# Attention values moved by 32 rows: sixteen transfers or sixty-four ScalarE copies

## The chip, the cores and the metric

The kernel runs on one core of a Trainium2 chip. The core has five instruction queues that run side by side and wait for each other through semaphores: TensorE (PE, matrix products), VectorE (DVE), ScalarE (ACT), GpSimd (POOL) and SyncE (SP, which here only issues transfers). Each queue works strictly in its own order. The metric is the device time of one execution in microseconds (us); lower is better.

## The reference

Two stages follow each other. The first is banded attention over 8 batches and 8 heads, 576 positions, head size 64. Heads 0 to 3 see the last 32 positions, heads 4 to 7 see 32 positions at a stride of 4. The second is a mixture of experts in which each of the 4608 tokens goes to one of 8 experts.

```python
mask_plain = (rel >= 0) & (rel < window)                                   # window = 32
mask_dil = (rel >= 0) & (rel < window * dilation) & (rel % dilation == 0)  # dilation = 4
attn = softmax(where(mask, q @ k.T / 8, -1e9)); x = attn @ v               # x: 4608 x 512
e_idx = argmax(x @ w_gate + modality_bias[modality_id])
out[t] = gate_w[t] * (relu(x[t] @ w1[e_idx[t]]) @ w2[e_idx[t]])
```

## The kernel before

**Attention.** The work is cut into 72 units, nine for each batch (`m` = 0 to 8). A unit computes 128 query rows of four heads; `kd` = 0 names the plain heads, `kd` = 1 the dilated ones. Units 0 to 3 are plain, unit 4 holds 64 rows of each, units 5 to 8 are dilated. A tile of 64 queries needs 96 keys: its own 64 and the 32 before them. The values of one batch and `kd` lie in a tile `vw` of 96 partitions: rows 32 to 95 of slot `i` hold the 64 values of tile `i`, rows 0 to 31 hold the last 32 values of tile `i - 1`. `load_v` (L123 to L132) fills rows 32 to 95 from device memory, with one transfer for `kd` = 0 and twelve for `kd` = 1. `shift_v` (L134) then fills rows 0 to 31 by moving rows 64 to 95 one slot on, inside the on-chip memory. Three `vw` tiles rotate.

**The loop.** At step `t` the loop (L940) emits, for each engine, pieces of several units: the scores of unit `t` (L340), the exponent of `t - 1` (L351), the transposed probabilities of `t - 2` (L356 on PE, the copy `pT` L359 on ACT), the product with the values of `t - 3` (`attend`, L365), the transposition of the result of `t - 4` (L387, `uxh` L391 on ACT, `uxl` L392 on DVE), the routing logits of `t - 5` (L411). In six of nine steps two `pieces` follow: transpositions of the next keys and queries (L294), which ACT copies out (L309, L311). PE, DVE, ACT and SP run in exactly this order; GpSimd's order is made by a scheduler, except for what goes through the object `pool`, which is kept in program order. The row-maximum subtraction `sm` runs there (L347, shown as L278, the helper's line).

**SP's queue.** Per batch it issues sixteen transfers of keys and queries (`st`, L116), thirteen of values (L127, L131) and two shifts (L137). The shift of `kd` = 1 is emitted at `m` = 3, that of the next batch's `kd` = 0 at `m` = 8.

**Routing.** After each batch a generator `gating` chooses the experts. Its product with `ewt` (L454) is a plain `nc.gpsimd` instruction, free to be placed by the scheduler. After batch 4 three expert slots of 256 tokens are full early. Their token rows are gathered by GpSimd (`xr`), go through device memory (`x_slot`, `xg`) and are transposed on DVE and split in two parts (`prepare_x`, L787 to L794).

**Mixture of experts.** `slots` (L817) runs 19 slots of eight blocks: products with `w1` (L855) and `w2` (L835), fed by splits of the weights on ACT and DVE (L803, L804). It starts in the step after the generator `background` has set `state['go']`, and is interleaved with the last attention units. That generator, for batch 4, gathers slot 0, runs `prepare_x`, waits for the last batch (`t` = 63), issues six groups of weight transfers, two yields apart, and then sets `go`. Since it is advanced twice a step, `prepare_x` before it delays what follows.

Of the kernel before, what the change touches and what calls it, by code (L numbers as in the profile page):

```python
# [15 lines left out]
ALU = mybir.AluOpType  # L16
# [6 lines left out]
B, H, S, D = 8, 8, 576, 64  # L23
# [4 lines left out]
WIN = 32  # L28
NCLS = 4
CL = S // NCLS  # L30
TQ = 64
NTILE = S // TQ
# [32 lines left out]
def kernel(  # L65
# [65 lines left out]
                nc.sync.dma_start(out=t[WIN + o:WIN + o + n, :, i, 0:D], in_=vv[r, j:j + n])  # L131
        return t  # L132

    def shift_v(b, kd):  # L134

        t = vw(b, kd)
        nc.sync.dma_start(out=t[0:WIN, :, 1:NTILE].rearrange("p h i d -> p h (i d)"),  # L137
                          in_=t[TQ:KW, :, 0:NTILE - 1].rearrange("p h i d -> p h (i d)"))

    state = {('qk', 0, 0): load_qk(0, 0, nc.scalar)}  # L140
    state['v', 0, 0] = load_v(0, 0)
# [20 lines left out]
    for m, kinds_of in enumerate(kinds):  # L162
        for u, kind in enumerate(kinds_of):
# [6 lines left out]
            if o is not None:  # L170
                mo = mt[:, 0:WIN + o]
                nc.gpsimd.affine_select(out=mo, in_=mo, pattern=[[0, WIN + o]], compare_op=ALU.is_ge,
                                        fill=-BIG, base=o - 1, channel_multiplier=-1)


    shift_v(0, 0)

    KC, FC = DM // P, FF // P
    w1q = [wraw.tile([P, KC, HALFF * P], F32, name=f"w1q{i}") for i in range(FC // HALFF)]
# [257 lines left out]
    def gating(b, lT):  # L437

        sh = [GB, NE, NGB]
        blk = slice(b * NGB, (b + 1) * NGB)  # L440
        lgp = psum['o'].tile([P, 512], F32, name="po")
        lg = lgp[0:GB, 0:NGB * 2 * NE].rearrange("p (c e) -> p e c", e=2 * NE)
        for c in range(NGB):
            nc.tensor.transpose(out=lg[:, :, c], in_=lT[:, GB * c:GB * (c + 1)], identity=ident[:2 * NE, :2 * NE])
        l = gwk.tile(sh, F32, name="l")
        nc.vector.tensor_tensor(out=l, in0=lg[:, 0:NE], in1=mterm[:, :, blk], op=ALU.add)
        nc.vector.tensor_tensor(out=l, in0=lg[:, NE:2 * NE], in1=l, op=ALU.add)
        mx = gwk.tile([GB, 1, NGB], F32, name="mx")
        nc.vector.tensor_reduce(out=mx[:, 0, :], in_=l.rearrange("p e c -> p c e"), op=ALU.max, axis=AX.X)
        mxb = mx.broadcast_to(sh)  # L450
        yield
        t0 = gwk.tile(sh, F32, name="t0")
        nc.vector.tensor_tensor(out=t0, in0=l, in1=mxb, op=ALU.is_equal)
        (nc.vector if b == B - 1 else nc.gpsimd).tensor_tensor(out=t0, in0=t0, in1=ewt, op=ALU.mult)  # L454
        ex = gwk.tile(sh, F32, name="ex")
        pool.tensor_tensor(out=ex, in0=l, in1=mxb, op=ALU.subtract)
        yield
        if b < B - 1:
            yield
        m2 = gwk.tile([GB, 1, NGB], F32, name="m2")  # L460
        nc.vector.tensor_reduce(out=m2[:, 0, :], in_=t0.rearrange("p e c -> p c e"), op=ALU.max, axis=AX.X)
        oh = gwk.tile(sh, BF16, name="oh")
        nc.vector.tensor_tensor(out=oh, in0=ewt, in1=m2.broadcast_to(sh), op=ALU.is_equal)
        nc.scalar.activation(out=ex, in_=ex, func=AF.Exp)
        yield
        sm_ = over_e(ex, "sume")
        pool.tensor_scalar(out=sm_, in0=sm_, scalar1=1e-9, scalar2=None, op0=ALU.add)

        rkp = psum['o'].tile([P, 512], F32, name="po")
        rk = rkp[0:GB, 0:NE * NGB].rearrange("p (e c) -> p e c", c=NGB)  # L470
        run = state['run']
        nc.tensor.matmul(out=rk, lhsT=upper, rhs=oh, start=True, stop=False)
        for c in range(NGB - 1):
            nc.tensor.matmul(out=rk[:, :, c + 1:], lhsT=ones_bf, rhs=oh[:, :, c:c + 1].broadcast_to([GB, NE, NGB - 1 - c]), start=False, stop=False)
        nc.tensor.matmul(out=rk, lhsT=ones_bf, rhs=run.broadcast_to(sh), start=False, stop=True)
        t1 = gwk.tile(sh, F32, name="t1")
        nc.vector.tensor_tensor(out=t1, in0=rk, in1=eoff, op=ALU.add)
        state['counts', b] = [run[:, :, 0]] + [oh[:, :, c] for c in range(NGB)]
        if b < B - 1:
            state['run'] = gwk.tile([GB, NE, 1], BF16, name="run")  # L480
            r3 = gwk.tile([GB, NE, 3], BF16, name="r3")
            pool.tensor_tensor(out=r3, in0=oh[:, :, 0:3], in1=oh[:, :, 3:6], op=ALU.add)
            for c in range(3):
                pool.tensor_tensor(out=state['run'], in0=run if c == 0 else state['run'], in1=r3[:, :, c:c + 1], op=ALU.add)
        yield
        pool.tensor_tensor(out=t1, in0=t1, in1=oh, op=ALU.mult)
        dst = gwk.tile([GB, NGB], I32, name="dst")
        yield
        nc.vector.tensor_copy(out=dst, in_=over_e(t1, "dstf"))
        nc.vector.reciprocal(out=pay[:, blk, 1].bitcast(F32), in_=sm_)  # L490
        scatters = state['scatters'] = []
        for c in range(NGB):
            if c > 0 and b < B - 1:
                yield
                if b not in round_of:
                    yield
            ins = nc.gpsimd.indirect_dma_start(out=table, out_offset=bass.IndirectOffsetOnAxis(ap=dst[:, c:c + 1], axis=0),
                                               in_=pay[:, b * NGB + c, :], in_offset=None).ins
            tc.add_manual_dep(ins, state['pool'].name, mybir.DependencyInfo(mybir.DependencyClass.NoSync, mybir.DependencyReason.SCHED_ONLY),
                              reason="GpSimd's order, but for the scatters among themselves")  # L500
            for before in scatters:
                tc.declare_no_dep(ins, before, reason="every token has a row of its own")
            for load in state['loads_of_ids']:
                tc.declare_no_dep(ins, load, reason="the rows of full slots are written before")
            scatters.append(ins)
        if b < B - 1:
            wait_all(scatters.pop(), scatters)
# [202 lines left out]
    def load_more(n, pieces):  # L710

        if n not in loads_of and n in si_of:
            loads_of[n] = [fetch_weights(si_of[n], n == 0), 0]
        if n in loads_of:
            for _ in range(min(pieces, 6 - loads_of[n][1])):
                next(loads_of[n][0], None)
                loads_of[n][1] += 1

    def background(b):


        if b < B - 1:
            yield
        steps = gating(b, state['lT', b])
        if b in round_of:
            for _ in steps:
                yield
                if ('counts', b) in state:
                    break
            yield from together(steps, slot_info(state['counts', b], round_of[b]))  # L730
            if round_of[b] > 0:
                return
            yield
            for n in range(2):
                fetch_slot(n)
                yield
            for _ in gather(0, ids_of[0]):
                yield
                yield
            for _ in range(4):  # L740
                yield
            yield from prepare_x(0, ids_of[0])

            while state['t'] < (B - 1) * 9:
                yield
            for _ in range(6):
                load_more(0, 1)
                yield
                yield
            while state['t'] < NU - 2:  # L750
                yield
            state['go'] = True
            return
        yield from steps
        if b == B - 1:
            yield
            yield from slot_info(state['counts', b], len(EARLY))
            yield from rest_info()
            state['routed'] = True
# [158 lines left out]
    for ch in qk_chunks(0, *state['qk', 0, 0]):  # L918
        ch()
    state['qk', 1, 0] = load_qk(1, 0)  # L920
    shift_v(0, 1)

    credit = 0.0

# [15 lines left out]
    for t in range(NU + LAG + 1):  # L940
# [10 lines left out]
        if t < NU:  # L951
            jobs = order[t][1]
            if m == 0:
                state['lT', b] = gwk.tile([2 * NE, S], F32, name="lT")
            if b + 1 < B:
                if m == 4:
                    pieces = qk_chunks(0, *state['qk', b + 1, 0])
                elif m == 8:
                    pieces = qk_chunks(1, *state['qk', b + 1, 1])
                    shift_v(b + 1, 0)  # L960
            if m == 0 and b > 0:
                load_v(b, 1, slice(6, None))
            elif m == 3:
                if b > 0:
                    shift_v(b, 1)
                if b + 1 < B:
                    state['v', b + 1, 0] = load_v(b + 1, 0)
            units.append(Unit(b, m, jobs, [state['v', b, 0], state['v', b, 1]] if m >= 4 else [state['v', b, 0]], state['lT', b]))
            units[t].scores()
# [20 lines left out]
        if 0 <= t - 4 < NU:  # L990
            units[t - 4].store()
            units[t - 4].keep(pool)
        for i in range(2):
            step()
            if i < len(pieces):
                pieces[i]()
# [56 lines left out]
```

## Time and profile before

| | |
|---|---|
| three timed executions | 732.46, 734.70, 734.91 us; median 734.7 us |
| the profiled execution | 731.71 us, of which 729.8 us is the span |
| first product of the mixture of experts | 279.55 us |
| last product of the mixture of experts | 711.5 us |
| mean granted TensorE clock | 0.926 |

The profile is one execution. A group's row reads: line, engine, operation, what it writes and reads, count, busy time, mean duration, and the idle time of the engine just before, with what ended it. A window's row gives, for a stretch of the span, each engine's busy time with its number of instructions, then the granted clock of TensorE as a share of full speed, the busy share of the transfer engines and the bytes they moved. A timeline row is start, duration, engine, line, operation and count, with the idle time before it in brackets. SP's rows are the times in which it was issuing.

### The profile page before, as it was taken

The page shows a single profiled execution, that of the slowest core. Times are in us where ns is not written, and L with a number is a line of the kernel's source. Part 1 is how long each engine was busy: PE and PEld are TensorE (multiplying, and loading weights), DVE is VectorE, ACT ScalarE, POOL GpSimd, SP SyncE. Part 2 cuts the span into 40 slices and gives each one's busy share as a digit, 9 for nine tenths or more (in the row PEclk, how much of TensorE's full clock was granted, in tenths as well). Part 3 has the DMA queues.
Part 4 walks back from the last instruction along what each step waited for, and adds up shares of the span by engine and source line. Part 5 has one row for each costly group of instructions (what it writes and reads, how often), then busy time and mean ns, then how long its engine had stood idle before and what let it go on. Part 6 is the DMA issues. An engine that isn't in the chain of part 4 may idle for free. (4 is left out here: it accounts for less than half of the span.)

```text
span 729.8 us, 17822 instructions
## 1 busy us (share of the span) xinstructions
PE 659.7 (90%) x6286; PEld 581.2 (80%) x6286; DVE 500.3 (69%) x1212; ACT 411.9 (56%) x900; POOL 292.1 (40%) x396
## 2 busy tenths in 40 slices
PE   5798789799687888989999999999999999999991
PEld 3686678687576767879999999998999999999980
DVE  1478579588586786786777666777666776667660
ACT  3476467477454544545656565566565666565550
POOL 7334557467465764564333133232132322220110
PEclk7599799799887868999999999999999999999996
DMA  9797796969967692423434583332323326831730
GB/s 161 134 220 174 161 197 154 211 141 188 185 140 165 183 239 76 101 73 111 123 95 124 169 223 87 102 116 74 102 73 102 116 75 164 239 92 54 189 93 12
DMA packets 165536, 99.20 MB, mean 136 GB/s; under 512 B 124400, under 2 KB 143346, under 8 KB 165444
## 3 DMA queue, kind: packets, MB, share of 16 engines
q1 hardware_dynamic: 148916, 68.15, 42.5%
q0 software_dynamic: 11120, 28.64, 12.8%
q10 hardware_dynamic: 5408, 1.24, 1.1%
q8 instruction: 51, 0.84, 0.5%
q14 instruction: 41, 0.34, 0.2%
HBM read 127.52 MB, written 29.39 MB: 215 GB/s over the span
## 5 line engine op out<-in xcount | busy, mean ns | idle before, releaser
L855 PE MATMUL pt<-xh,w1l 128*128 128x256 f32 (+1 forms) x608 | 172.5, 284 | 3.2 <-DVE w1l L804 3.2
L855 PE MATMUL pt<-xl,w1h 128*128 128x256 f32 (+1 forms) x608 | 172.3, 283 | 0.0
L855 PE MATMUL pt<-xh,w1h 128*128 128x256 f32 (+1 forms) x608 | 172.2, 283 | 0.1
L861 ACT ACTIVATE hh<-pt 128x256 fp32r<-128x256 f32 (+1 forms) x152 | 57.6, 379 | 165.7 <-PE pt L855 165.7
L278 POOL DMA_INDIRECT xr<-x_dram,idt x74 | 84.6, 1144 | 122.9 <-DMA x_slot<-xr 83.9
L804 DVE TENSOR_TENSOR w2l<-w2q,w2h 128x512 fp32r<-128x512 f32 x152 | 104.9, 690 | 41.3 <-ACT w2h L803 33.1
L855 PEld LDWEIGHTS pt<-xh,w1h 128*128 128x128 f32 x608 | 116.7, 192 | 7.0 <-ACT w1h L803 0.4
L855 PEld LDWEIGHTS pt<-xl,w1h 128*128 128x128 f32 x608 | 116.8, 192 | 5.7
L855 PEld LDWEIGHTS pt<-xh,w1l 128*128 128x128 f32 x608 | 116.6, 192 | 4.0 <-DVE w1l L804 4.0
L835 PE MATMUL py<-w2h,hh 128*128 128x512 f32 x296 | 117.6, 397 | 0.0
L835 PE MATMUL py<-w2h,hl 128*128 128x512 f32 x296 | 116.8, 395 | 0.0
L835 PE MATMUL py<-w2l,hh 128*128 128x512 f32 x296 | 116.0, 392 | 0.0
L862 DVE SCALAR_TENSOR_TENSOR hl<-pt,hh 128x256 fp32r<-128x256 f32 (+1 forms) x152 | 63.4, 417 | 75.7 <-ACT hh L861 75.6
L278 POOL DMA_INDIRECT out_dram<-ys,idt x37 | 39.2, 1059 | 177.7 <-ACT ys L838 115.0
L804 DVE TENSOR_TENSOR w1l<-w1q,w1h 128x512 fp32r<-128x512 f32 x152 | 103.9, 684 | 1.8 <-ACT w1h L803 1.7
L803 ACT CAST w1h<-w1q 128x512 fp32r<-128x512 f32 x152 | 94.5, 622 | 2.3 <-DMA w1q<-in_moe_w_dram 2.3
L803 ACT CAST w2h<-w2q 128x512 fp32r<-128x512 f32 x152 | 93.1, 612 | 0.1
L359 ACT COPY pT<-pt 96x512 f32<-96x512 f32 x72 | 41.8, 581 | 89.3 <-PE pt L356 88.3
L365 PE MATMUL po<-vw,pT 96*64 96x65 f32 x1152 | 58.3, 247 | 28.3 <-DMA vw<-vw 19.5
L278 POOL TENSOR_TENSOR sm<-sm,nmx 128x384 f32<-128x384 f32 x72 | 59.8, 831 | 55.6 <-DVE den L372 32.3
L365 PEld LDWEIGHTS po<-vw,pT 96*64 96x64 f32 x1152 | 46.7, 155 | 40.3 <-issue 13.9
L835 PEld LDWEIGHTS py<-w2l,hh 128*128 128x128 f32 x296 | 55.7, 188 | 13.2
(159 smaller groups left out, 1114.2 us busy)
## 6 DMA issues: line engine op xcount, KB each, us to landing
w2q<-in_moe_w_dram SPq DMA_DIRECT2D x76, 512.0 KB
w1q<-in_moe_w_dram SPq DMA_DIRECT2D x152, 256.0 KB
st<-in_k_dram SPq DMA_DIRECT2D x64, 144.0 KB
x_slot<-xr SPq DMA_DIRECT2D x18, 512.0 KB
xg<-x_slot SPq DMA_DIRECT2D x72, 128.0 KB
x_dram<-x_sb POOLq DMA_DIRECT2D x32, 256.0 KB
st<-in_q_dram SPq DMA_DIRECT2D x56, 144.0 KB
vw<-in_v_dram SPq DMA_DIRECT2D x8, 576.0 KB
```

Source lines behind the costliest of these rows:

```text
L278: ins = tc.keep_in_program_order(getattr(nc.gpsimd, name)(*args, **kw))
L359: nc.scalar.copy(out=self.pT, in_=src)
L365: nc.tensor.matmul(out=pov[u * TQ:(u + 1) * TQ, h, :], lhsT=self.pT[:, h, u * TQ:(u + 1) * TQ], rhs=self.vts[kd][:, h, i, :], start=True, ...
L803: nc.scalar.copy(out=hi, in_=raw)
L804: nc.vector.tensor_tensor(out=lo, in0=raw, in1=hi.bitcast(F32), op=ALU.subtract)
L835: nc.tensor.matmul(out=py[u], lhsT=ht[:, us], rhs=wt, start=(f + n == 0), stop=(f + n == FC + 1))
L855: nc.tensor.matmul(out=ph, lhsT=wt[:, c, :], rhs=xt[:, c, 0:cols], start=(c + i == 0), stop=(c + i == KC + 1))
L861: nc.scalar.activation(out=hh, in_=ph, func=AF.Relu)
L862: nc.vector.scalar_tensor_tensor(out=hl, in0=ph, scalar=0.0, in1=hh.bitcast(F32), op0=ALU.max, op1=ALU.subtract)
```

## The change

`shift_v` no longer issues a transfer. It copies the 32 rows of one head with one ScalarE instruction, and the loop calls it once per step, between `store` and the `pieces`: heads 0 to 3 of `kd` = 1 at `m` = 3 to 6, heads 0 to 3 of the next `kd` = 0 at `m` = 8, 0, 1 and 2 (for the first batch two heads at `t` = 0 and two at `t` = 1). The product with `ewt` goes through `pool`. In `background`, `prepare_x` no longer stands ahead of the weight transfers but beside their second half.

```diff
-    def shift_v(b, kd):
+    def shift_v(b, kd, h):
 
         t = vw(b, kd)
-        nc.sync.dma_start(out=t[0:WIN, :, 1:NTILE].rearrange("p h i d -> p h (i d)"),
-                          in_=t[TQ:KW, :, 0:NTILE - 1].rearrange("p h i d -> p h (i d)"))
+        nc.scalar.copy(out=t[0:WIN, h, 1:NTILE].rearrange("p i d -> p (i d)"), in_=t[TQ:KW, h, 0:NTILE - 1].rearrange("p i d -> p (i d)"))
...
-        (nc.vector if b == B - 1 else nc.gpsimd).tensor_tensor(out=t0, in0=t0, in1=ewt, op=ALU.mult)
+        (nc.vector if b == B - 1 else pool).tensor_tensor(out=t0, in0=t0, in1=ewt, op=ALU.mult)
...
             for _ in gather(0, ids_of[0]):
                 yield
                 yield
-            for _ in range(4):
-                yield
-            yield from prepare_x(0, ids_of[0])
 
             while state['t'] < (B - 1) * 9:
                 yield
-            for _ in range(6):
+            for _ in range(3):
                 load_more(0, 1)
                 yield
+                yield
+            steps = prepare_x(0, ids_of[0])
+            for i in range(6):
+                if i % 2 == 0:
+                    load_more(0, 1)
+                next(steps, None)
                 yield
...
+        if 3 <= m <= 6 and b < B:
+            shift_v(b, 1, m - 3)
+        elif t < NU and (m == 8 and b + 1 < B or m < 3):
+            for h in ((m + 1) % 9,) if t > 2 else {0: (0, 1), 1: (2, 3), 2: ()}[t]:
+                shift_v(b + (m == 8), 0, h)
```

The four calls of the old `shift_v` (ahead of the loop, at `m` = 3 and at `m` = 8) go. The instructions move in three places. First, ScalarE's queue in a batch from `m` = 3 on: the row maximum's exponent `pe`, the copy `pT`, `uxh`, and the key and query copies `kT`, `qT`. Before:

```order
L351 ACTIVATE pe<-sm 128x384
L359 COPY pT<-pt 96x512
L391 CAST uxh<-pt 128x256
L351 ACTIVATE pe<-sm 128x384
L359 COPY pT<-pt 96x512
L391 CAST uxh<-pt 128x256
L311 COPY kT_101<-pt 128x2x2x96
L309 ACTIVATE qT_100<-po 128x2x2x96
```

and with the change:

```order
L347 ACTIVATE pe<-sm 128x384
L355 COPY pT<-pt 96x512
L387 CAST uxh<-pt 128x256
L137 COPY vw_106<-vw_106 32x520
L347 ACTIVATE pe<-sm 128x384
L355 COPY pT<-pt 96x512
L387 CAST uxh<-pt 128x256
L137 COPY vw_106<-vw_106 32x520
L307 COPY kT_101<-pt 128x2x2x96
L305 ACTIVATE qT_100<-po 128x2x2x96
```

A copy now stands behind `uxh` in eight of nine steps, ahead of the key and query copies. The transfers of SP's queue keep their order without the shifts.

Second, GpSimd's queue in batch 6, where the routing of batch 5 meets the gathers `xr` of slot 0. The number of a tile grows with the place of its instruction in the program; `t0` is the product with `ewt`. Before:

```order
L278 TENSOR_TENSOR sm_4181<-sm_4181,nmx_4182 128x384
L454 TENSOR_TENSOR t0_4347<-t0_4347,ewt_268 96x48
L278 TENSOR_TENSOR ex_4350<-l_4304,mx_4307 96x48
L278 DMA x_dram0_84<-x_sb_4212 128x2x256
L278 DMA xr_4215<-x_dram0_84,idt_4146 128x256
L278 DMA x_dram1_85<-x_sb_4065 128x2x256
L278 TENSOR_TENSOR sm_4235<-sm_4235,nmx_4236 128x384
L278 DMA xr_4215<-x_dram1_85,idt_4146 128x256
L278 TENSOR_TENSOR sm_4310<-sm_4310,nmx_4311 128x384
```

and with the change:

```order
L274 TENSOR_TENSOR sm_4219<-sm_4219,nmx_4220 128x384
L274 DMA xr_4253<-x_dram0_84,idt_4184 128x256
L274 DMA x_dram1_85<-x_sb_4102 128x2x256
L274 TENSOR_TENSOR sm_4274<-sm_4274,nmx_4275 128x384
L274 DMA xr_4253<-x_dram1_85,idt_4184 128x256
L274 TENSOR_TENSOR sm_4350<-sm_4350,nmx_4351 128x384
L274 DMA xr_4253<-x_dram0_84,idt_4184 128x256
L274 TENSOR_TENSOR t0_4387<-t0_4387,ewt_267 96x48
L274 TENSOR_TENSOR ex_4390<-l_4344,mx_4347 96x48
```

The product stood ahead of two `sm` of earlier steps and stands behind them now; the first gather stands ahead of them.

Third, TensorE's queue at the end of attention: the last scores (`pss`), and the first products of the mixture of experts (`pt<-xh,w1h`). Before:

```order
L340 MATMUL pss<-kT_103,qT_102 64x96 x8
L365 MATMUL po<-vw_104,pT 64x65 x8
L411 MATMUL po<-uxh,wgs 16x128
L411 MATMUL po<-uxl,wgs 16x128
L411 MATMUL po<-uxh,wgs 16x128
L411 MATMUL po<-uxl,wgs 16x128
L356 MATMUL pt<-ident,pe 96x128 x4
L387 MATMUL pt<-ident,x_sb 128x128 x2
L365 MATMUL po<-vw_104,pT 64x65 x8
```

and with the change:

```order
L336 MATMUL pss<-kT_103,qT_102 64x96 x8
L361 MATMUL po<-vw_104,pT 64x65 x8
L407 MATMUL po<-uxh,wgs 16x128
L407 MATMUL po<-uxl,wgs 16x128
L407 MATMUL po<-uxh,wgs 16x128
L407 MATMUL po<-uxl,wgs 16x128
L854 MATMUL pt<-xh,w1h 128x256
L854 MATMUL pt<-xl,w1h 128x256
L854 MATMUL pt<-xh,w1l 128x256
```

The mixture of experts begins two steps earlier, in the step of the last scores: `go` is set at `t` = 70 instead of 72. The first weight transfers are issued at `t` = 63 instead of 66.

More of the change, by code (lines that the diff above doesn't have):

```diff
@@ L173 @@
                                         fill=-BIG, base=o - 1, channel_multiplier=-1)
-    shift_v(0, 0)
     KC, FC = DM // P, FF // P
@@ L920 @@
     state['qk', 1, 0] = load_qk(1, 0)
-    shift_v(0, 1)
     credit = 0.0
@@ L959 @@
                     pieces = qk_chunks(1, *state['qk', b + 1, 1])
-                    shift_v(b + 1, 0)
             if m == 0 and b > 0:
@@ L963 @@
             elif m == 3:
-                if b > 0:
-                    shift_v(b, 1)
                 if b + 1 < B:
```

## The prediction

> **What bounds the kernel now.** I read the page first, for the engines and the granted clock.
>
> ```profile
> span 729.8 us, 17822 instructions
> PE 659.7 (90%) x6286; PEld 581.2 (80%) x6286; DVE 500.3 (69%) x1212; ACT 411.9 (56%) x900; POOL 292.1 (40%) x396
> PEclk7599799799887868999999999999999999999996
> ```
>
> TensorE is busy for 90% of the span. Its clock is full from slice 16 on (a slice is 18.2 us) and broken before. The change touches only what lies before, the attention stage and its end. So the second view is the windows: the batches 1 to 7 from first score to first score (the last without its ninth unit), then that unit and the start of the experts.
>
> ```profile
> core 0: us, PE busy (x) PEld busy (x) DVE busy (x) ACT busy (x) POOL busy (x), PEclk, DMA share, GB/s
> 49.50:83.70 34.20, 27.28 (x448) 23.41 (x447) 23.40 (x77) 18.83 (x48) 14.86 (x26) 0.85 0.89 190
> 83.70:111.70 28.00, 26.04 (x444) 22.31 (x443) 22.95 (x75) 18.93 (x47) 18.37 (x29) 0.94 0.84 177
> 111.70:144.70 33.00, 27.57 (x449) 23.67 (x447) 23.11 (x77) 19.24 (x48) 19.99 (x32) 0.84 0.84 178
> 144.70:171.20 26.50, 25.10 (x448) 21.27 (x447) 22.30 (x73) 18.77 (x47) 17.30 (x27) 1.00 0.86 165
> 171.20:204.50 33.30, 26.68 (x451) 22.67 (x450) 23.32 (x81) 19.06 (x47) 19.06 (x31) 0.90 0.94 181
> 204.50:242.10 37.60, 30.14 (x445) 25.64 (x444) 27.28 (x95) 19.33 (x47) 23.44 (x34) 0.82 0.64 155
> 242.10:271.10 29.00, 24.57 (x370) 20.38 (x369) 22.95 (x70) 14.23 (x39) 20.41 (x30) 0.76 0.87 206
> 271.10:284.00 12.90, 9.72 (x111) 8.56 (x111) 7.78 (x26) 4.78 (x12) 9.42 (x12) 0.74 0.42 121
> ```
>
> Batch 4 took 26.5 us, with TensorE 25.1 us busy at full clock: there TensorE is the bound. Batches 1 to 5 do the same work and took 34.2, 28.0, 33.0, 26.5 and 33.3 us, together 155.0. Five times 26.5 would be 132.5. What lies between, 22.5 us, is idle TensorE and lost clock. The waits of TensorE name the cause, and the timeline places it.
>
> ```profile
> PE po L365 <- DMA vw<-vw: 19.5, 7, 5.9
> 76.80 0.99 PE L365 MATMUL po<-vw,pT 96*64 96x65 f32 x13 [5.23 <-DMA vw<-vw]
> 105.88 0.65 PE L365 MATMUL po<-vw,pT 96*64 96x65 f32 x14 [1.54 <-DMA vw<-vw]
> 137.41 0.88 PE L365 MATMUL po<-vw,pT 96*64 96x65 f32 x11 [5.01 <-DMA vw<-vw]
> 106.40:109.80 3.40, 3.40 (x42) 2.75 (x40) 1.82 (x9) 1.27 (x3) 0.84 (x2) 0.50 1.13 280
> 133.70:144.00 10.30, 6.59 (x68) 5.77 (x68) 3.71 (x14) 1.55 (x4) 3.55 (x6) 0.50 1.07 209
> ```
>
> The shift is waited for 19.5 us in all, mostly at m = 7, where unit 4 is the first to need kd = 1. Each wait also costs clock: after 1.54 us of idling the clock is 0.50 for 3.4 us, around the 5.01 us for 10.3 us.
>
> Why the shift is late stands in SP's queue of batch 1.
>
> ```profile
> 53.80 9.67 SPq L131 DMA_DIRECT2D vw<-in_v_dram  x12
> 63.99 2.65 SPq L116 DMA_DIRECT2D st<-in_k_dram  x4
> 69.42 0.71 SPq L137 DMA_DIRECT2D vw<-vw  x1
> L137 SPq DMA_DIRECT2D vw<-vw x16: 615/688/1662, 14.4 to 248.6; - x16
> vw<-vw SPq DMA_DIRECT2D x16, 260.0 KB
> ```
>
> The queue issues back to back. The shift, emitted at m = 3, is issued at 69.42 behind eight loads, about when TensorE reaches m = 6, and TensorE goes on at 76.80: 7.4 us after the issue. With the transfer engines 84 to 94% busy in these batches, supply is nearly as scarce as TensorE.
>
> **The change part by part.** Sums are made against the profiled 731.7 us (729.8 of span, 1.9 around it); the median of the timed runs, 734.7, stands 3 us higher, and I add 2 to 3 at the end.
>
> *What the copy costs.* No row shows a ScalarE copy between on-chip tiles of 32 x 520. These are the nearest.
>
> ```profile
> L803 ACT CAST w2h<-w2q 128x512 fp32r<-128x512 f32 x152 | 93.1, 612 | 0.1
> L359 ACT COPY pT<-pt 96x512 f32<-96x512 f32 x72 | 41.8, 581 | 89.3 <-PE pt L356 88.3 <-PE po L411 0.5 <-ACT pe L351 0.5
> L311 ACT COPY kT<-pt 128x384 f32<-128x384 f32 x24 | 20.6, 860 | 1.8 <-PE pt L294 1.7
> L351 ACT ACTIVATE pe<-sm 128x384 f32<-128x384 f32 x72 | 38.0, 528 | 18.9 <-POOL sm L278 18.8
> ```
>
> Bounds are 0.58 us (pT) and 0.86 us (kT, whose output is strided). The copy runs over contiguous elements, as w2h does, from the same kind of memory, so I take 0.62 us. 64 copies are 39.7 us (37 to 55), eight to a batch are 5.0. ACT rises from 18.8 to 23.8 us in a batch of 26.5, and the row of pT shows that it waited 88.3 us for TensorE: most copies lie in that time. Two places do not. With key and query copies (m = 4 to 6) ACT gets 0.53 + 0.58 + 0.37 (uxh, quoted below) + 2 x 0.86 (kT, and qT of the same shape) + 0.62 = 3.8 us of summed durations, where a unit of batch 4 takes 26.5 / 9 = 2.9. Neighbours overlap somewhat, so 0.2 to 0.3 us are lost, three times. And at m = 3 the product with the values needs the copy made at the end of m = 2: about 0.4 us. I take 1 us a batch; the bounds are 0, all hidden, and 5.0, none.
>
> *Which wait takes the place of the old one.* ACT is in order, and the copy must wait for the values to land. For kd = 1 it stands at m = 3, four units before TensorE needed the transfer. Behind it are queued the next exponent, pT, and so all of TensorE two units on. The profile lets me place it.
>
> ```profile
> 61.23 0.37 ACT L391 CAST uxh<-pt 128x256 fp32r<-128x256 f32 x1
> 94.00 0.37 ACT L391 CAST uxh<-pt 128x256 fp32r<-128x256 f32 x1
> 182.07 0.37 ACT L391 CAST uxh<-pt 128x256 fp32r<-128x256 f32 x1
> 82.38 8.53 SPq L131 DMA_DIRECT2D vw<-in_v_dram  x12
> 173.50 9.55 SPq L131 DMA_DIRECT2D vw<-in_v_dram  x12
> ```
>
> These are the ends of m = 3 in batches 1, 2 and 5. ACT would be there at 61.6, 94.4 and 182.4; SP had issued the last values at 63.5, 90.9 and 183.1. A transfer lands some 3 to 7 us after that (the shift took 7.4), so the values would come about 5 to 9, 0 to 4 and 4 to 8 us late. Less the two shifts in front of them on SP (0.69 us each) and their traffic, say 3 us late on average. TensorE still has the scores, the product and the transpositions of one unit to do in that time, near 2 us, so it waits about 1.2 us a batch instead of 19.5 / 5 = 3.9. Gain in five batches: 13.5 us. Bounds: 0, the wait is inherited whole, and 19.5.
>
> *The clock.* In the two half-clock windows quoted TensorE was busy 3.40 and 6.59 us, half of it lost; the other two long waits of batches 1 to 5 are like them, so near 10 us lost. Shorter waits keep some windows: gain 6.5, bounds 0 and 10. Batches 1 to 5 thus give 13.5 + 6.5 - 5 = 15 us, 28 us a batch. The ideal was 22.5.
>
> [...]
>
> *GpSimd's product in batch 6.*
>
> ```profile
> 224.91 0.28 POOL L454 TENSOR_TENSOR t<-t,ewt 96x48 f32<-96x48 f32 x1 [5.50 <-DVE t L453]
> 228.33 0.84 POOL L278 TENSOR_TENSOR sm<-sm,nmx 128x384 f32<-128x384 f32 x1
> 226.45 1.10 POOL L278 DMA_INDIRECT xr<-x_dram,idt  x1 [0.30 <-issue]
> 230.25 1.14 PE L365 MATMUL po<-vw,pT 96*64 96x65 f32 x16 [5.01 <-ACT pT L359]
> 219.49 0.39 SPq L626 DMA_DIRECT2D idt<-table  x1
> ```
>
> The product, placed two units early, holds GpSimd 5.5 us; `sm` behind it comes at 228.33, and TensorE idles 5.01 us and loses clock. Now `xr` stands first. Its ids are issued at 219.49 and need 2 to 3 us, then come `xr` (1.1) and a store: `sm` near 225.5, some 3 us earlier. With the clock I take 5 us; bounds 0 (the ids are as late as the product was) and 10.
>
> *prepare_x moved by three units.* In batch 7 DVE stands at its transposition until the gathered rows land, and TensorE behind it.
>
> ```profile
> 252.01 0.71 DVE L787 STREAM_TRANSPOSE xt<-xg 128x512 f32<-128x512 f32 x1 [1.57 <-DMA xg<-x_slot]
> 253.08 0.23 PE L411 MATMUL po<-uxl,wgs 128*16 128x128 f32 x1 [1.89 <-DVE uxl L392]
> 253.20:266.80 13.60, 11.91 (x133) 9.60 (x132) 10.80 (x30) 5.25 (x13) 9.03 (x12) 0.50 1.03 246
> ```
>
> Then the clock is 0.50 for 13.6 us with TensorE busy 11.9, 6 us lost. The rows have landed three units later. But GpSimd is 20.4 us busy in those 29.0, now with three gathers in a row (3.3 us) ahead of one `sm`, so another wait is likely. I take 3.5; bounds 0 and 8.
>
> *The experts two steps earlier.* In the last window TensorE is idle 3.2 us and the clock is 0.74. Products of the first slot now fill this. Their weights come three units earlier. Gain 3, bounds 0 and 6. What covers the later routing of batch 7 is the three early slots; without that cover slot 3 would wait.
>
> In batch 0 no shift is waited for (the first such wait is in batch 1): 0. The sum is 15 + 5 + 3.5 + 3 = 26.5, so 705.2 for a profiled execution, and with the 2 to 3 us to the median **707.5 us**.
>
> **The rivals.**
>
> *ACT inherits the wait.* The values come 5 us late on average, as in batches 1 and 5 above, and the stall only moves to m = 3. For it: SP's lag. Against: the two shifts leave the queue. Then batches 1 to 5 gain at most 3, the rest 11.5: 720.
>
> *Supply decides.* By bytes: the rate of 165 to 190 GB/s is some 5.5 MB a batch, the two shifts are 0.52 MB, 9.5% or 2.9 us, 15 us in five batches: the forecast again. By SP's issue time, 1.4 us a batch, 7 us: 715.
>
> *All batches run as batch 4.* 22.5 from batches 1 to 5 and 8, 6, 4 from the others: 694. Against it: 23.8 us of ACT in 26.5.
>
> [...]
>
> *Slower.* Both copies wait in each batch, that of kd = 0 at m = 8 too. From 5.5 us of lateness at both places the 7 us a batch that could be saved are eaten (2 x (5.5 - 2) = 7); at 8 us each, batches 1 to 5 lose 25 and the others gain 11.5: 748. For kd = 0 there is little sign of it: the old shift was issued at m = 8 with hardly a wait on the values.
>
> *The transfers were hidden anyway* is ruled out by 19.5 us of named waits; the change removes all sixteen.
>
> **How the numbers follow.** The forecast has 0.54; inherited wait 0.13, supply by issue 0.10, all as batch 4 0.13, the clock rule 0.04, slower 0.06 (a sixth of it within 0.5%). The range 692 to 727 takes in the first five with their bounds. What a measurement can tell from no change is about 0.5%, 3.7 us, so faster is below 731. Faster 0.89, the same 0.06 (an inherited wait with little of the other gains), slower 0.05.
>
> **What would show it.** Right: no wait on `vw<-vw`; copies of 0.60 to 0.65 us; ACT waiting for `in_v_dram` at m = 3, 5 to 15 us in all; batches 1 to 5 near 28 us; L454's wait below 1 us; the first expert product in the step of the last scores; from there the same 430 us. Wrong: copies near 0.9 us, ACT waits above 25 us, a batch above 31 us, or a wait of slot 3 for its rows.

## The result and the profile after

Four executions of the changed kernel took 712.21, 713.95, 715.94 and 717.60 us, median 714.95. The kernel before, beside it, had a median of 733.58 us. The ratio is 0.9744, with a 95% interval of 0.9706 to 0.9782: 18.6 us faster, where 27.2 were predicted. Ratios, here and below, leave out executions in the chip's slower state (one of before, 740.70 us, and one of short copies, 720.86), so one can differ a little from the quotient of two medians. The profiled execution is the longest of the four (717.6), while that of before is one of its short ones (731.7), so the two traces differ by 14.1 us only.

The page of the changed kernel, its span, TensorE and the clock in 40 slices:

```profile
span 715.9 us, 17885 instructions
PE 652.0 (91%) x6286; PEld 572.8 (80%) x6286; DVE 496.2 (69%) x1212; ACT 455.5 (64%) x964; POOL 290.7 (41%) x396
PEclk7699999999789899989999999999999999999996
```

ScalarE is busy 43.6 us longer, TensorE 7.7 us shorter for the same 6286 products, at a mean granted clock of 0.954 instead of 0.926. The windows of the changed kernel are cut as before, from first score to first score: batches 0 to 7 (the last without its ninth unit).

```profile
core 0: us, PE busy (x) PEld busy (x) DVE busy (x) ACT busy (x) POOL busy (x), PEclk, DMA share, GB/s
14.10:45.70 31.60, 26.26 (x356) 21.38 (x356) 20.07 (x61) 21.99 (x47) 11.45 (x15) 0.76 0.97 184
45.70:72.50 26.80, 24.66 (x449) 21.21 (x447) 22.25 (x75) 24.54 (x55) 13.58 (x24) 1.00 0.81 186
72.50:101.70 29.20, 25.37 (x448) 21.24 (x447) 22.38 (x76) 24.40 (x55) 19.03 (x30) 1.00 0.82 170
101.70:128.40 26.70, 24.67 (x444) 21.15 (x443) 22.43 (x76) 24.44 (x55) 18.91 (x30) 1.00 0.87 183
128.40:156.30 27.90, 25.69 (x448) 21.62 (x446) 22.37 (x76) 24.64 (x55) 19.01 (x30) 1.00 0.82 159
156.30:192.20 35.90, 29.23 (x455) 25.28 (x454) 23.18 (x80) 24.52 (x55) 19.06 (x30) 0.86 0.77 148
192.20:224.20 32.00, 27.95 (x446) 23.53 (x445) 25.48 (x94) 24.88 (x55) 22.50 (x34) 0.89 0.58 140
224.20:256.20 32.00, 23.35 (x370) 19.30 (x369) 23.68 (x74) 19.81 (x47) 22.27 (x32) 0.87 0.95 212
```

Batches 1 to 4 run at full clock, two of them in 26.7 and 26.8 us, with 24.5 us of ScalarE inside. Batch 5 is longer than before (33.3). The table sets what each stretch did in these two executions against the sum of the prediction. The last row counts from the scores of the last unit to the end of the last product with `w1`.

| stretch | before, us | after, us | moved | predicted |
|---|---|---|---|---|
| batch 0 | 35.5 | 31.6 | -3.9 | 0 |
| batches 1 to 5 | 155.1 | 146.5 | -8.6 | -15 |
| batches 6 and 7 (to the last unit) | 66.6 | 64.0 | -2.6 | -8.5 |
| last unit to the last `w1` product | 440.7 | 441.6 | +0.9 | -3 |

Where a wait went, the waits of TensorE in the changed kernel say first (total, times, longest):

```profile
PE po L361 <- ACT pT L355: 16.5, 14, 5.3
PE pt L854 <- DVE w1l L803: 7.5, 5, 5.2
```

No wait on `vw<-vw` is left, of 19.5 us. In its place stand waits for `pT`, the copy of ScalarE, and for `w1l`, the weight split of VectorE. The row of the copies in the groups by line, and then their waits in ScalarE's timeline:

```profile
L137 ACT COPY vw<-vw 32x520 f32<-32x520 f32 x64 | 39.7, 624 | 13.7 <-DMA vw<-in_v_dram 10.6 <-DMA st<-in_k_dram 1.7
```

```profile
87.27 0.62 ACT L137 COPY vw<-vw 32x520 f32<-32x520 f32 x1 [2.76 <-DMA vw<-in_v_dram]
141.90 0.63 ACT L137 COPY vw<-vw 32x520 f32<-32x520 f32 x1 [0.92 <-DMA vw<-in_v_dram]
175.21 0.62 ACT L137 COPY vw<-vw 32x520 f32<-32x520 f32 x1 [6.88 <-DMA vw<-in_v_dram]
```

A copy takes 624 ns and all take 39.7 us, the predicted figure. ScalarE waits 10.6 us for values, but not 2 us in each batch: 6.88 of it falls at one place, in batch 5. TensorE idles behind it (timelines of TensorE), and again in batch 7 and in the second expert slot:

```profile
176.90 1.14 PE L361 MATMUL po<-vw,pT 96*64 96x65 f32 x16 [5.33 <-ACT pT L355]
234.30 1.13 PE L361 MATMUL po<-vw,pT 96*64 96x65 f32 x16 [3.34 <-ACT pT L355]
308.07 0.58 PE L854 MATMUL pt<-xh,w1l 128*128 128x256 f32 x1 [5.23 <-DVE w1l L803]
```

The stall of batch 7 comes from GpSimd (its timeline):

```profile
228.63 1.09 POOL L274 DMA_INDIRECT xr<-x_dram,idt  x1 [0.30 <-DVE uxl L388]
230.03 1.02 POOL L274 DMA_INDIRECT xr<-x_dram,idt  x1 [0.30 <-DVE den L369]
231.35 1.01 POOL L274 DMA_INDIRECT xr<-x_dram,idt  x1 [0.30 <-issue]
232.38 0.84 POOL L274 TENSOR_TENSOR sm<-sm,nmx 128x384 f32<-128x384 f32 x1
```

Three gathers of slot 1 hold one `sm` for 3.7 us. That of the expert slot comes from VectorE (its timeline; between 299.64 and 306.68 stand 35 more short instructions of the list of slots and one `hl`):

```profile
299.04 0.68 DVE L803 TENSOR_TENSOR w1l<-w1q,w1h 128x512 fp32r<-128x512 f32 x1
299.64 0.15 DVE L523 TENSOR_SCALAR cn<-po 1x8 int32<-1x8 f32 x1
...
306.68 0.14 DVE L598 TENSOR_TENSOR info_h<-ec 1x1 int32<-1x1 f32 x1
306.74 0.67 DVE L803 TENSOR_TENSOR w2l<-w2q,w2h 128x512 fp32r<-128x512 f32 x1
307.35 0.67 DVE L803 TENSOR_TENSOR w1l<-w1q,w1h 128x512 fp32r<-128x512 f32 x1
```

The list of slots that the last batch's routing makes takes 7.1 us in a row, and the next split of weights stands behind it.

### The profile page after: what moved, and what is told of

It reads as the page before. It is cut to its first block, busy times and chain, and to the rows that moved or that the text cites. A ratio compares the mean times of both kernels' runs of the same rounds, so it can differ in the third digit from the quotient of the medians.

```text
span 715.9 us, 17885 instructions
## 1 busy us (share of the span) xinstructions
PE 652.0 (91%) x6286; PEld 572.8 (80%) x6286; DVE 496.2 (69%) x1212; ACT 455.5 (64%) x964; POOL 290.7 (41%) x396
## 3 DMA queue, kind: packets, MB, share of 16 engines
q10 hardware_dynamic: 5408, 1.24, 1.1%
## 5 line engine op out<-in xcount | busy, mean ns | idle before, releaser
L274 POOL DMA_INDIRECT xr<-x_dram,idt x74 | 82.8, 1118 | 121.4 <-DMA x_slot<-xr 70.5
L274 POOL TENSOR_TENSOR sm<-sm,nmx 128x384 f32<-128x384 f32 x72 | 59.9, 832 | 64.4 <-DVE den L368 49.3
L361 PE MATMUL po<-vw,pT 96*64 96x65 f32 x1152 | 55.9, 239 | 20.3 <-ACT pT L355 16.5
L361 PEld LDWEIGHTS po<-vw,pT 96*64 96x64 f32 x1152 | 44.6, 147 | 32.7 <-ACT pT L355 20.9
L834 PEld LDWEIGHTS py<-w2h,hh 128*128 128x128 f32 x296 | 56.4, 190 | 6.7
```

Of the source, the lines that this page charges most:

```text
L274: ins = tc.keep_in_program_order(getattr(nc.gpsimd, name)(*args, **kw))
L361: nc.tensor.matmul(out=pov[u * TQ:(u + 1) * TQ, h, :], lhsT=self.pT[:, h, u * TQ:(u + 1) * TQ], rhs=self.vts[kd][:, h, i, :], start=True, ...
L834: nc.tensor.matmul(out=py[u], lhsT=ht[:, us], rhs=wt, start=(f + n == 0), stop=(f + n == FC + 1))
```

## The experiments

Theory A after this reading: the copies bring the gain, nearly all in batches 0 to 5; the other two parts are taken back by later waits. Theory B, the prediction's: each part brings its own term.

All ten runs in one view. Ratios are to the kernel before on the same chip, with 95% intervals. The columns behind are of each profiled execution, in us, cut as in the table above; "slots" is the time of the first two expert slots, "start" that from the last unit's scores to the first expert product.

| kernel | median | ratio | batch 0 | 1 to 5 | 6, 7 | last unit to end | start | slots |
|---|---|---|---|---|---|---|---|---|
| before | | 1 | 35.5 | 155.1 | 66.6 | 440.7 | 8.4 | 53.5 |
| the change | 714.95 | 0.974 (0.971 to 0.978) | 31.6 | 146.5 | 64.0 | 441.6 | 2.1 | 60.1 |
| copies alone | 718.95 | 0.979 (0.972 to 0.986) | 30.9 | 143.7 | 69.8 | 441.6 | 8.5 | 53.4 |
| product alone | 733.88 | 1.000 (0.996 to 1.003) | 33.9 | 157.2 | 66.9 | 442.6 | 8.6 | 54.9 |
| experts alone | 737.10 | 1.004 (1.001 to 1.007) | 34.3 | 156.5 | 67.1 | 446.6 | 1.8 | 64.6 |
| copies and product | 715.51 | 0.973 (0.970 to 0.976) | 32.1 | 140.6 | 68.2 | 441.9 | 8.2 | 53.8 |
| late copies | 715.40 | 0.976 (0.969 to 0.983) | 33.0 | 140.5 | 63.5 | 443.7 | 1.7 | 62.4 |
| early loads | 713.27 | 0.972 (0.966 to 0.978) | 32.4 | 139.6 | 65.3 | 441.5 | 1.8 | 60.8 |
| short copies | 711.81 | 0.965 (0.956 to 0.974) | 31.0 | 136.1 | 66.4 | 445.0 | 1.8 | 64.4 |
| late ids | 716.78 | 0.978 (0.971 to 0.985) | 31.4 | 142.6 | 59.6 | 448.8 | 1.8 | 68.3 |
| split list | 712.73 | 0.970 (0.965 to 0.975) | 32.7 | 140.6 | 64.3 | 442.3 | 2.0 | 59.7 |
| early loads, split list | 711.12 | 0.972 (0.967 to 0.977) | 31.4 | 141.9 | 62.1 | 439.4 | 1.8 | 57.9 |

### Which part brings the gain

Four kernels: each part alone on the kernel before, and the change without the experts' part. Copies alone:

```diff
 def shift_v(b, kd, h):          # and its calls, as in the change; nothing else of it
+        nc.scalar.copy(out=t[0:WIN, h, 1:NTILE]..., in_=t[TQ:KW, h, 0:NTILE - 1]...)
```

> The copies alone: the shifts are copies as in the change, the product with the gate weights and the preparation of slot 0 are as before. Theory A (the traces of before and after, cut by batch: batch 0 -4.0 us, batches 1 to 5 -8.5, and the copies also bring the three row gathers of slot 1 two units earlier on GpSimd, which costs 3 in batch 7): about 9 to 12 us faster than before, 722 to 725. ScalarE waits for the values near the ends of m = 3, 5 to 15 us in all, and in batch 7 a maximum subtraction stands behind three gathers with TensorE idle about 3 us. Theory B (most of the gain is the experts' earlier start and the product): 4 us faster or less, 730.

Measured: 718.95, 15.5 us faster; 15.9 come from batches 0 to 5 of its trace, batch 7 loses 3.5 (32.5 instead of 29.0). The gain is larger than either theory said.

The product alone:

```diff
-        (nc.vector if b == B - 1 else nc.gpsimd).tensor_tensor(out=t0, in0=t0, in1=ewt, op=ALU.mult)
+        (nc.vector if b == B - 1 else pool).tensor_tensor(out=t0, in0=t0, in1=ewt, op=ALU.mult)
```

> The routing product in program order alone, all else as before. Theory A (the prediction's step): batch 6 loses its 5 us stall at its seventh unit, 4 to 6 us faster, 728 to 730. Theory B (the ids and the gathers are as late as the product was, or the gain of batch 6 in the changed kernel came from the copies): within 1.5 us of before.

Measured: no change. But batch 6 does gain, 29.5 instead of 37.6 us, and batch 7 loses as much, 37.5 instead of 29.0. The windows of batches 6 and 7 of this kernel, and then a row each of its VectorE and TensorE timelines in batch 7:

```profile
205.50:235.00 29.50, 25.07 (x444) 21.12 (x443) 23.25 (x85) 19.54 (x48) 21.31 (x31) 1.00 0.72 166
235.00:272.50 37.50, 23.16 (x373) 19.18 (x373) 23.34 (x73) 14.71 (x39) 21.59 (x31) 0.82 0.87 199
```

```profile
254.44 0.71 DVE L787 STREAM_TRANSPOSE xt<-xg 128x512 f32<-128x512 f32 x1 [9.72 <-DMA xg<-x_slot]
255.52 0.29 PE L411 MATMUL po<-uxl,wgs 128*16 128x128 f32 x1 [10.53 <-DVE uxl L392]
```

The transposition of slot 0 had waited 1.57 us for its rows; now it waits 9.72, since the units come sooner and the rows do not: SP issues their loads (`xg`) at 244.18 instead of 245.28, behind the same twelve value loads, and they are there at 254.44 instead of 252.01. In the kernel before, the product's stall covered that wait.

The experts' part alone:

```diff
-            for _ in range(4):
-                yield
-            yield from prepare_x(0, ids_of[0])
...
+            steps = prepare_x(0, ids_of[0])      # beside the weight transfers, as in the change
```

> The preparation of slot 0 beside its weight transfers and the start two steps earlier alone, all else as before. Theory A (the changed kernel's trace: the first expert product comes 6.3 us sooner behind the last scores, but slot 1 takes 6.6 us longer, because VectorE does the last batch's routing list between two weight splits): within 2 us of before, with a wait of TensorE for a w1 split of 4 us or more in slot 1. Theory B (the prediction's 3 + 3.5 us from the start and the transposition): 5 to 7 us faster, 727 to 729.

Measured: 0.4% slower (0.1 to 0.7%). The first expert product comes 6.7 us sooner behind the last scores, and the first two slots take 11.1 us longer. TensorE's timeline has the same stall as the changed kernel:

```profile
327.41 0.58 PE L858 MATMUL pt<-xh,w1l 128*128 128x256 f32 x1 [5.21 <-DVE w1l L807]
```

Copies and product, with the start as before (the diff is the change's without the lines of `background`):

> The changed kernel without the new preparation of slot 0: copies and product, start as before. Theory A (the earlier start is taken back in slot 1): as fast as the changed kernel within 2 us, 713 to 717, and no wait of 5 us for a w1 split. Theory B (the earlier start is worth its 6 us): 719 to 722.

Measured: 715.51 us, the same as the change. Its start is 6.1 us later and its first two slots are 6.3 us shorter; TensorE waits 1.5 us in all for `w1l`. So the copies carry the gain, the experts' part none, and the product none alone. That the product is worth something beside the copies (715.51 against 718.95) can't be told: the intervals overlap.

### What the copies cost, and ScalarE's wait for the values

```diff
-        if 3 <= m <= 6 and b < B:
-            shift_v(b, 1, m - 3)
+        if 5 <= m <= 6 and b < B:
+            for h in (2 * m - 10, 2 * m - 9):
+                shift_v(b, 1, h)
```

> The changed kernel with the four copies of kd = 1 two by two at m = 5 and 6 instead of one by one at m = 3 to 6; the values get two more units, some 6 us, to land. Theory A (the one long batch among 4 and 5, 33 to 36 us instead of 27 in three kernels with copies, is ScalarE's wait for the values, 5 to 7 us, and the half clock behind it): no wait of ScalarE on in_v_dram above 1 us, no batch 1 to 5 above 30 us, 5 to 8 us faster than the change: 707 to 710, ratio 0.964 to 0.968. Theory B (two copies beside the key and query copies overload ScalarE at m = 5 and 6 by about 1.3 us a batch, or the values are later than that): 712 to 717, no faster than the change.

Measured: the trace is as A says: no wait on `in_v_dram`, no batch of 1 to 5 above 28.8 us. The time is not: 715.4. The four batches ahead pay for it; they took 28.5, 27.8, 27.7 and 27.7 us where copies and product, with single copies, took 26.8, 26.7, 26.8 and 27.1. Two copies in a step cost about 1 us a batch, as B said.

```diff
-            if m == 0 and b > 0:
-                load_v(b, 1, slice(6, None))
...
+            elif m == 7:
+                state['v', b + 1, 1] = load_v(b + 1, 1, slice(0, 6))   # ahead of the queries
...
             elif m == 8:
-                state['v', b + 1, 1] = load_v(b + 1, 1, slice(0, 6))
+                load_v(b + 1, 1, slice(6, None))
```

> The changed kernel with the values of kd = 1 issued one unit sooner on SyncE: the first six transfers at m = 7, ahead of the queries, the other six at m = 8. Theory A (what is late is the issue, which stands behind the key and query transfers and their buffers): ScalarE's wait on in_v_dram goes, no batch 1 to 5 above 30 us, 707 to 710. Theory B (the bytes are what is scarce, and whatever goes first makes the rest late): TensorE waits for the keys and queries (st) instead, 713 to 718.

Measured: 713.27, in theory B's range. The trace bears out neither in full: no batch of 1 to 5 is above 29.2 us, as A said, but ScalarE still waits 5.8 us for values, in three pieces of at most 2.8; and TensorE has no wait for keys or queries in these batches, which was B's sign. The last kernel below has the same loads, and a batch of 31.6 us behind a wait of 4.5 us in its trace, so that this order removes the long batch isn't shown.

```diff
+        n = NTILE if 2 * b + kd < 3 else 2
-        nc.scalar.copy(out=t[0:WIN, h, 1:NTILE]..., in_=t[TQ:KW, h, 0:NTILE - 1]...)
+        nc.scalar.copy(out=t[0:WIN, h, 1:n]..., in_=t[TQ:KW, h, 0:n - 1]...)
```

> What the copies cost: from the dilated heads of batch 1 on each copy moves one slot (32 x 65) instead of eight (32 x 520), which leaves out seven eighths of the shift there and 0.35 to 0.4 us of ScalarE each, some 23 us in all; the waits and the order are the same. Theory A (the prediction's 1 us a batch): 4 to 6 us faster than the change in seven batches, 709 to 711. Theory B (hidden, batches 1 to 4 are 26.7 to 27.9 us with 24.5 us of ScalarE in them and TensorE still the bound): within 2 us of the change, 713 to 717.

Measured: 711.81, between the two theories, with an interval (0.956 to 0.974) that overlaps the change's (0.971 to 0.978). The windows of batches 2 to 4 are sharper. With short copies, and then those of copies and product:

```profile
71.60:96.60 25.00, 24.57 (x444) 21.19 (x443) 22.45 (x76) 21.90 (x55) 19.07 (x30) 1.00 0.78 171
96.60:122.50 25.90, 24.83 (x449) 21.26 (x447) 23.00 (x77) 21.82 (x55) 19.39 (x31) 1.00 0.86 176
122.50:149.70 27.20, 24.98 (x444) 21.18 (x443) 23.00 (x78) 21.61 (x54) 19.43 (x30) 1.00 0.82 179
```

```profile
73.10:99.80 26.70, 24.62 (x444) 21.13 (x443) 22.54 (x76) 24.44 (x55) 18.97 (x30) 1.00 0.89 180
99.80:126.60 26.80, 24.76 (x448) 21.22 (x447) 22.61 (x76) 24.52 (x55) 18.92 (x30) 1.00 0.79 169
126.60:153.60 27.00, 24.93 (x444) 21.22 (x443) 22.39 (x76) 24.33 (x55) 18.88 (x30) 1.00 0.89 170
```

TensorE has the same 24.8 us of work in both, all at full clock; 2.5 to 2.7 us less of ScalarE make a batch 0.8 us shorter on average (78.1 against 80.5 for the three), though unevenly: by 1.7, 0.9 and -0.2 us. The average is near the 1 us that the prediction gave a whole set of eight copies, for somewhat over half their time; three batches of one execution each can't say it more closely.

### Batch 7 and the start of the experts

```diff
-            for n in range(2):
-                fetch_slot(n)
+            fetch_slot(0)
...
+            fetch_slot(1)                # after the preparation of slot 0
             while state['t'] < NU - 2:
```

> The changed kernel with the ids of slot 1 fetched at the end of attention instead of two batches sooner, so that GpSimd's scheduler can't put the three gathers of slot 1 ahead of a maximum subtraction in batch 7. Theory A (these gathers are batch 7's stall of 3.3 us and its half clock): batch 7 to its last unit 27 to 29 us instead of 32, 710 to 712. Theory B (the rows of slot 1 then come late, and slot 1 is held, or another wait of batch 7 takes over): 714 to 720.

Measured: both. Batches 6 and 7 take 59.6 us, the least of all kernels, and batch 7 28.9 us, with no gather of slot 1 in it: the gathers were its stall. Then slot 0 takes 35.5 us instead of 27.0, and the time is 716.78.

The last two kernels cut the list of slots:

```diff
+            state['listing'] = True              # as the list begins
             yield from slot_info(state['counts', b], len(EARLY))
...
         step(1)
         advance()
-        advance()
+        if 'listing' not in state:
+            advance()
```

> The changed kernel, but while the last batch's list of slots is made on VectorE (38 short instructions, 7.1 us between two weight splits) the routing is advanced once per expert step instead of twice, so that a pair of splits stands in its middle. Theory A (this uncut list is what takes the earlier start back: slot 1 takes 32.7 to 33.3 us in every kernel with the early start, 26.4 to 28.0 in every one without): slot 1 back to 27 to 29 us, the wait of 5.2 us for w1l gone, 4 to 6 us faster than the change, 709 to 711, ratio 0.966 to 0.969. Theory B (the time from the last unit's scores to the end is 441 to 444 us in all kernels but three, whatever the start, because VectorE and the work of attention's end bound it): slot 1 gains what a later wait takes, 713 to 716.

> The same with the values of kd = 1 issued one unit sooner, as in the run with early loads (713.3). Theory A: both gains add, 706 to 709. Theory B: as that run, 712 to 714.

Measured: 712.73, and 711.12 with the early loads. In the first, the wait of 5.2 us is gone, but TensorE waits in smaller pieces instead; the four longest (its timeline):

```profile
295.46 0.39 PE L855 MATMUL pt<-xh,w1l 128*128 128x256 f32 x1 [1.04 <-DVE w1l L804]
299.69 0.39 PE L855 MATMUL pt<-xh,w1l 128*128 128x256 f32 x1 [1.16 <-DVE w1l L804]
305.45 0.58 PE L855 MATMUL pt<-xh,w1l 128*128 128x256 f32 x1 [2.69 <-DVE w1l L804]
331.95 0.39 PE L855 MATMUL pt<-xh,w1l 128*128 128x256 f32 x1 [0.95 <-DVE w1l L804]
```

Its waits for `w1l` come to 7.1 us, against 7.5 in the change, and from the last unit to the end it takes 442.3 against 441.6. So the mechanism of theory B held: the list's work on VectorE is paid, cut or uncut. The second kernel lies just below its theory B; the gains of A, 706 to 709, did not add. Both have lower medians than the change, but on their chip the kernel before is faster too (731.80 against 733.58), and all intervals overlap; that they beat the change is not shown.

## Why the prediction was right, and where it was not

The sign was right and the time lies in the range; the size was 18.6 us instead of 27.2. The copies brought what was forecast of them, a little less; the terms that failed are the product and the experts' part. In the two traces these terms (5, 3.5 and 3 us) came to 1.7 us together, while batch 0, put at nothing, gave 3.9: that the total is no further off is partly luck. Two of the prediction's own signs also came out against it: a batch took more than 31 us (batch 5, 35.9), and from the first expert product to the last with `w1` it took 439.5 us instead of "the same 430" (432.2 before). By its steps:

- **The price of a copy**: right, 0.62 us predicted, 0.624 measured. The 1 us a batch for the copies on the path is supported by the short copies (0.8 us a batch for 2.5 to 2.7 us less of ScalarE). ScalarE came to 24.5 us a batch (23.8 predicted) and did not become the bound.
- **ScalarE's wait for the values**: the total was right (10.6 us, predicted 5 to 15), the form was not. Instead of "1.2 us a batch" there is little in most batches and one wait of 4.8 to 6.9 us in batch 4 or 5, in all six kernels with single copies and the loads of the change (for four of them `in_v_dram` is named). SP's rows of the changed kernel show the lag grow:

```profile
101.40 7.57 SPq L131 DMA_DIRECT2D vw<-in_v_dram  x12
127.80 10.72 SPq L131 DMA_DIRECT2D vw<-in_v_dram  x12
158.32 13.04 SPq L131 DMA_DIRECT2D vw<-in_v_dram  x12
```

  The values of batch 5 begin 30.5 us after those of batch 4 and take 13 us to issue, while the units before them ran at 26.7 to 29.2 us a batch. Here the queue was a little slower than the units, and with its lead used up that was paid once, with 6.88 us. That supply is the cause of this one wait is the reading of these rows; no run took the bytes away.
- **Batches 1 to 5**: 15 us predicted. The profiled execution of the change gained 8.6, but the four other kernels with single full copies and the same loads (copies alone, copies and product, late ids, split list) took 143.7, 140.6, 142.6 and 140.6 us, a gain of 11.3 to 14.5. In these the step was 0.5 to 3.7 us too large; in the change's own trace, whose batch 5 is 2.5 us longer than the longest batch of the four, 6.4.
- **Batch 0**: predicted 0, gained 3.9 here. It took 30.9 to 33.0 us in all nine kernels with copies, 33.9 to 35.5 in the three without. No shift is waited for there, but the shifts stood ahead of the first loads on SP. SP's rows before, and with the change:

```profile
14.38 0.67 SPq L137 DMA_DIRECT2D vw<-vw  x1
16.18 10.97 SPq L131 DMA_DIRECT2D vw<-in_v_dram  x12
27.25 2.60 SPq L116 DMA_DIRECT2D st<-in_k_dram  x4
```

```profile
14.02 10.76 SPq L131 DMA_DIRECT2D vw<-in_v_dram  x12
24.90 2.60 SPq L116 DMA_DIRECT2D st<-in_k_dram  x4
```

  The key loads (`st`) come 2.4 us sooner. The issue of the first shift took 0.67 us, yet the queue went on 1.8 us after its start. The step "no shift is waited for: 0" looked at TensorE's waits alone and not at the queue. The earlier loads are not all of the 3.9 us, though. The window of batch 0 before, beside the first row of the windows above:

```profile
13.90:49.50 35.60, 28.85 (x360) 24.01 (x360) 20.30 (x61) 17.00 (x39) 11.66 (x15) 0.66 0.96 171
```

  TensorE is busy 2.6 us less with the change, at a clock of 0.76 instead of 0.66, and idle 1.4 us less. Whether the earlier loads bring the clock as well, no run shows.
- **GpSimd's product**: 5 us predicted, failed as a gain of its own. The wait did go: in the changed kernel the product follows the third gather without one.

```profile
216.08 1.02 POOL L274 DMA_INDIRECT xr<-x_dram,idt  x1 [0.16 <-issue]
217.12 0.30 POOL L274 TENSOR_TENSOR t<-t,ewt 96x48 f32<-96x48 f32 x1
```

  What was left out is the next wait: the product alone gained 8.1 us in batch 6 and lost 8.5 in batch 7, on rows that land no sooner. The prediction named what is late next for the copies, and not here.
- **prepare_x moved**: 3.5 us predicted, and batch 7 became 3.0 us longer. The transposition no longer waits for its rows, as said. But "three gathers in a row ahead of one `sm`" was seen and priced as "another wait is likely" inside the 3.5; it cost 3.34 us and a half clock of 6.8 us, and late ids, which moves these gathers away, gives batch 7 back 3.1 us. The earlier preparation costs time there even without the copies (experts alone: batch 7 takes 31.5 us instead of 29.0, with these gathers where they were); why, no run shows. Nor were the gathers new, as the "now" of the prediction has it: in the kernel before, four gathers in a row (250.29 to 255.28) stood ahead of one `sm` in batch 7, two `sm` later, where the transposition was waiting too. GpSimd's scheduler places the gathers: they run ahead of `sm` that come long before them in the program. With the copies and the change's own loads it puts them two `sm` sooner than before. The tile numbers of the changed kernel show how far out of program order that is:

```
xr_5256<-x_dram0_84,idt_4215 128x256     (three of these)
sm_4647<-sm_4647,nmx_4648 128x384
```

  So what goes through the object `pool` is not kept in program order throughout, as the description of the kernel had it.
- **The experts two steps earlier**: 3 us predicted, failed. They start 6.3 us sooner (2.1 us behind the last scores instead of 8.4), and the first two slots take 6.6 us longer. "What covers the later routing is the three early slots" was the wrong cover: the third and fourth slots take their 22.6 us each, so slot 3 did not wait for its rows; but the routing itself runs on VectorE, between the weight splits that TensorE now needs. From the last unit to the end, 439.4 to 442.6 us stand in eight of the twelve kernels, whichever start they have; the four above that (443.8 to 448.8) all have the early one.
- **The rivals**: not all batches run as batch 4 of the kernel before (two of five do, 26.7 and 26.8 us); an inherited wait would have left batches 1 to 5 a gain of at most 3 us, and they gained 8.6, in the others 11.3 to 14.5, which refutes it, and slower too. The clock rule, given 0.04, is shown by no run: in the changed kernel half clock stands behind 3.41, 1.86 and 1.35 us of idling (rows in the last section). Supply by issue time, 715, has the right number: its 7 us in batches 1 to 5 are near the 8.6 of the change's trace, but not near the others', and its 11.5 us elsewhere did not come. Supply by bytes gave the forecast's own 15 us; no run tells it apart from the forecast, because every kernel with copies both drops the old wait and moves 0.52 MB a batch less.

Open stays what fixes the 441 us behind the last unit, some 12 more than nineteen slots of 22.56 us, and which transfer makes the values late in batch 4 or 5.

## What to carry to other kernels

A transfer that a busy queue issues late can be worth replacing by a short copy on an engine with idle time (here 15.5 us for the copies alone); look at the queue's own rows too, since what stood behind the transfer came sooner as well (the key loads of batch 0 by 2.4 us). A stall that was removed ahead of a wait for something that did not come sooner only moved there (with the product alone batch 6 gained 8.1 us and batch 7 lost 8.5): before a gain is counted, find what the next step waits for and whether that arrives earlier. And work that was started earlier gained nothing where an engine it shares still had the same chores to do in between (the experts began 6.3 us sooner, and their first two slots took 6.6 us longer).

## What the hardware showed beside that

**Half clock began on a grid of 3.41 us, mostly behind 1.6 us or more of idling.** In the twelve traces all starts of half clock behind the first lie on a grid of 3413.3 ns, and their lengths, but for the last, which the end of the execution cuts, are multiples of it, to within 1.1 ns (162 values). I cut each trace by its grid from 40 us to 700 us, took the intervals at full clock, and counted how often half clock followed, by how long TensorE was idle in the interval, as the profile has its products' ends:

| idle in the interval, us | intervals | followed by half clock |
|---|---|---|
| under 0.8 | 1999 | 2 |
| 0.8 to 1.15 | 75 | 1 |
| 1.15 to 1.3 | 18 | 5 |
| 1.3 to 1.6 | 22 | 7 |
| 1.6 to 2.0 | 21 | 18 |
| over 2.0 | 39 | 39 |

In this count an interval idle for over 2.0 us (0.59 of it) was always followed by half clock, and one idle for a third of it (1.15 to 1.3 us) in 5 of 18 cases. Three windows of the changed kernel, with half clock behind 3.41, 1.86 and 1.35 us of idling:

```profile
175.90:186.20 10.30, 9.30 (x88) 8.56 (x89) 6.37 (x22) 8.90 (x18) 3.02 (x6) 0.51 1.09 168
199.90:206.80 6.90, 6.90 (x85) 5.64 (x84) 5.38 (x16) 4.95 (x12) 3.39 (x5) 0.51 0.64 132
254.50:258.00 3.50, 3.50 (x44) 2.90 (x42) 2.59 (x11) 2.06 (x5) 2.08 (x6) 0.51 0.98 266
```

A wait of 2.17 us before 245.55, which a grid point cut in two (0.93 and 1.24 us of idling in the intervals on either side), cost no clock, while the shorter waits of 1.86 and 1.35 us were followed by 6.8 and 3.4 us of half clock. Nor did one busy interval always end it: behind 199.94 TensorE is busy for all of two grid intervals (6.90 of the 6.90 us above) at half clock.

**ScalarE moved 32 partitions to 32 others (64 to 95 into 0 to 31) at about the price of a cast that stays in its partitions**: 624 ns for 520 elements, against 612 ns for the 512 of `w2h`.
